# An attention and gating kernel on one core: a rewritten order table, work moved from GpSimd to VectorE, and the inverse transform's third products split off

## The chip, the cores and the metric

The kernel runs on one core of one Trainium2 chip. The metric is the device time of one execution in microseconds (us), the median of a few runs. Lower is better. The engines are called as the profile calls them: PE (TensorE, matrix products; PEld is its weight load), DVE (VectorE), ACT (ScalarE), POOL (GpSimd) and SP (the engine that issues most DMA transfers; its queue is SPq).

## What is computed

Two layers, one behind the other. The first is a linear attention with a learned feature map; the second projects the attention's output three ways, convolves one of the projections with a filter along the sequence by way of a Fourier transform, multiplies the three, and projects once more.

```python
# q, k, v: (8, 8, 576, 64); w_phi: (64, 128)
def phi(x):
    proj = einsum('bhsd,df->bhsf', x, w_phi)
    proj = proj - max(abs(proj), axis=-1)
    return concatenate([exp(proj), exp(-proj)], axis=-1)
q_p, k_p = phi(q), phi(k)
kv = einsum('bhsf,bhsd->bhfd', k_p, v)
num = einsum('bhsf,bhfd->bhsd', q_p, kv)
den = einsum('bhsf,bhf->bhs', q_p, sum(k_p, axis=2)) + 1e-06
x = (num / den) -> (8, 576, 512)          # heads side by side
x1, x2, x3 = split(x @ w_proj, 3)         # w_proj: (512, 1536)
conv = irfft(rfft(x2, axis=1) * rfft(filter, axis=0), axis=1)
out = (x1 * conv * x3) @ w_out            # (8, 576, 512), float32
```

## The kernel before

**An order written out by hand.** The program has no loops over batches that set its order. A long table of words, `PLAN`, is walked once, and each word calls one method with its arguments: `Pk,2,0@0` calls `Pk(2, 0)` with PSUM bank 0. A word issues between one and 72 instructions of one engine. So `PLAN` fixes, for each engine, the order of its instructions; each engine then runs its own list in that order and waits on semaphores where an input or a buffer is not ready. Nothing is moved at run time: an instruction that waits holds back all that stands behind it on its engine. The order of the words that belong to different engines against each other matters only where it decides which of two uses of a buffer comes first.

**One batch.** The 8 batches run through the same stages, overlapped by hand; a batch's words carry its number `b` first.

- Loads: `load,q,b`, `load,k,b`, `load,v,b` (line 596) are issued by POOL, with a cast from float32 to bf16 on the way. Batch 0 is loaded in four halves for q and k instead (`loadh`, line 602). The three column blocks of `w_proj` are loaded by POOL as `w_load,proj,0` to `2` (line 586); block 0 feeds the words `X1`, block 1 `X2`, block 2 `X3`.
- `trh,k,b,X` and `trh,q,b,X` (line 608) transpose one half of k or q by DMA, issued by SP. Batch 0's are transposed on PE (`pt`, line 618) and copied out of PSUM by `pte` on ACT or DVE.
- `Pk` and `Qn` (lines 636, 643) multiply by `w_phi`; `maxk` and `maxq` (DVE, line 716) take the largest magnitudes; `ex` (ACT, line 698) takes the exponentials, 128x1024 at a time. `mhi`, `mlo`, `trm`, `trme` turn the maxima of q so that `Pq` (lines 670, 676) can subtract them in PSUM.
- `em` (ACT) writes the factors of v, and `vs` (line 758) scales v by them: four words per batch, `p` and `m`, two halves X. `KV` (line 773) sums k against scaled v, `KVe` copies it out, `NE` and `NEt` (lines 787, 796) multiply by q, `rc` and `xn` (DVE) divide.
- `trx` (SP, line 825) transposes the attention's output for the projections `X1` and `X3` (line 917). `f1` and `f2` (lines 854, 860) are the two stages of folds, sums and differences of bf16 blocks of 128x512, ahead of the forward Fourier products `Ft` and `Fs` (lines 869, 876). `Fe` and `Xl` copy the spectrum out, `X2` (line 895) projects it, `Y1` (DVE) multiplies by the filter's spectrum into four tiles `T0` to `T3` and a leftover tile `T4`; `m3` (line 909) adds them in pairs.
- `I` (line 970) is the inverse transform of one block of 128 features: six matmuls of 288 columns, three for the even and three for the odd half. `Ie`, `Ip`, `Im` bring it out, `ym` (line 1005) multiplies by the other two projections, `O` (line 1016) is the last projection, `Oe` copies it out, `st` stores it.

**Two shapes of product on PE.** Some words work on 64 rows of the array and pair two halves of a tile (`Pk`, `Qn`, `Pkt`, `Qnt`, `Pq`, `Pqt`, `KV`, `Ft`); the profile writes `64*128` for them. The rest use all 128 rows (`128*128`).

**The third pair of `I`.** `T4` holds the leftover frequencies, 64 rows of the even and 64 of the odd half; the tile `inv` holds zeros in the rows of the other half. So `I` multiplies all 128 rows of `T4` once for each half.

**Set-up.** Before the first batch POOL writes index tables (`gi_nr`, `gi_fr` and others, lines 322 to 342), DVE and ACT turn them into angles (`ang`, `frac`) and sines (`sin`), which are the transform's matrices. The filter is loaded by SP (`fl_load`), folded by POOL (`fa`, line 495) into `fs`, and transformed once (`Ff`, `Ffe`, `H`, `He`). `fs` lies in the memory of `turn`, the tile that the sines are computed from. `wz` are products of zeros that fill PE early on. After the set-up, `late` gives its memory to the tiles of the second layer.

Of the kernel before, what the change touches and what calls it, by code (L numbers as in the profile page):

```python
# [36 lines left out]
fl_load,1,1 pt,k,0,1,1@7 exz ex,k,m,0,1@2 maxk,0,0@4 maxq,0,1@0 fl_load,3,1 fl_load,2,0 ex,k,p,0,0@4
pt,k,0,1,0@0 load,v,0 ex,k,m,0,0@4 pt,q,0,1,1@1 load,k,1 fl_load,3,0 maxk,0,1@2 pte,ACT,k,0,1,1@7
fl_load,1,0 pte,DVE,q,0,1,0@6 pte,ACT,k,0,1,0@0 Qn,0,0@4 pte,ACT,q,0,1,1@1 load,q,1 fa,POOL,0
maxq,0,0@4 Pkt,0@6 Qn,0,3@0 trh,k,1,0 maxkt,0@6 ex,k,p,0,1@2 wz,24@4 wz,17@2 trh,q,1,0 Qnt,0@4  # L40
maxq,0,3@0 fa,POOL,1 em,p,0,0 exkt,p,0@6 Pk,0,2@0 exkt,m,0@6 Qn,0,2@2 ex,k,p,0,2@0 maxqt,0@4
Pk,0,3@6 maxq,0,2@2 em,m,0,0 ex,k,m,0,3@6 w_load,proj,2 mhi,0 ex,k,p,0,3@6 rev@4 maxk,0,2@0
vs,POOL,p,0,0 mlo,POOL,0 vs,POOL,m,0,0 ex,k,m,0,2@0 trm,0@2 trme,DVE,0@2 Pq,0,0@2 ex,q,p,0,0@2
Pq,0,1@0 maxk,0,3@6 fb,0@4 em,m,0,1 em,p,0,1 vs,POOL,p,0,1 fb,1@4 wz,11@6 wz,9@7 KV,0,0@6
ex,q,p,0,1@0 ex,q,m,0,1@0 ex,q,m,0,0@2 Pq,0,3@4 Pq,0,2@0 ex,q,m,0,3@4 KVe,DVE,0,0@6 vs,POOL,m,0,1
NE,0,0@6 rc,0,0@6 NE,0,1@2 xn,0,0@6 trh,q,1,1 ex,q,p,0,3@4 Ff,2@6 Pk,1,1@4 rc,0,1@2 xn,0,1@2
f1,POOL,0,0,0 maxk,1,1@4 ex,q,p,0,2@0 Ffe,ACT,2@6 KV,0,1@2 Qn,1,0@6 ex,q,m,0,2@0 wz,5@0
KVe,ACT,0,1@2 ex,k,m,1,1@4 Pk,1,0@2 maxq,1,0@6 ex,k,p,1,1@4 maxk,1,0@2 NE,0,3@0 rc,0,3@0 Ff,3@6
Ffe,ACT,3@6 NE,0,2@4 xn,0,3@0 trh,k,1,1 w_load,proj,0 ex,k,m,1,0@2 Ff,1@6 rc,0,2@4 ptx,0,3@0
xn,0,2@4 ex,k,p,1,0@2 ptx,0,0@1 ptxe,DVE,0,0@1 ptx,0,2@4 f1,POOL,0,0,1 ptxe,DVE,0,3@0 Qnt,1@2  # L50
ptxe,ACT,0,2@4 Ffe,ACT,1@6 maxqt,1@2 Pqt,0@0 exqt,p,0@0 exqt,m,0@0 Qn,1,3@4 Ff,0@6 Ffe,ACT,0@6
Qn,1,2@2 maxq,1,3@4 Pk,1,2@0 Qn,1,1@4 load,v,1 maxq,1,2@2 ex,k,m,1,2@0 maxq,1,1@4 trx,0,1 X1,0,3@6
load,k,2 Pkt,1@2 ex,k,p,1,2@0 w_load,proj,1 maxk,1,2@0 exkt,m,1@2 X1,0,2@7 maxkt,1@2 X1,0,1@4
X1e,ACT,0,2@7 X1e,ACT,0,3@6 mhi,1 NEt,0@0 H,0@5 rct,0@0 xnt,0,1@0 X3,0,1@6 H,3@7 X1e,ACT,0,1@4
f1,POOL,0,1,1 f1,POOL,0,1,0 em,p,1,0 xnt,0,0@0 f2,POOL,0,1,0 tm,0,1@6 load,q,2 f2,POOL,0,1,1
exkt,p,1@2 Ft,0,1,0@2 He,DVE,3,0@7 Fs,0,2@2 Hl,ACT He,DVE,3,1@7 Fs,0,3@0 X1,0,0@4 Fe,ACT,0,2@2
Fe,ACT,0,3@0 Ft,0,0,6@2 He,DVE,0,0@5 X1e,ACT,0,0@4 He,DVE,0,1@5 Pk,1,3@0 f2,POOL,0,0,0 f2,POOL,0,0,1
Fs,0,1@6 Fe,DVE,0,1@6 Fs,0,0@2 H,1@4 ex,k,m,1,3@0 Fe,ACT,0,0@2 He,ACT,1,1@4 X3,0,2@5 He,ACT,1,0@4
mlo,POOL,1 trm,1@6 maxk,1,3@0 em,m,1,0 Xl,DVE,0 trme,DVE,1@6 em,p,1,1 X3,0,0@7 H,2@2 X2,0,2@3
em,m,1,1 ex,k,p,1,3@0 tm,0,0@7 H,4@4 trh,k,2,0 He,DVE,4,0@4 tm,0,2@5 vs,POOL,p,1,0 Pq,1,0@6  # L60
He,ACT,2,0@2 X3,0,3@0 tm,0,3@0 ex,q,m,1,0@6 vs,POOL,m,1,0 KV,1,0@4 vs,POOL,p,1,1 trxt,0
vs,POOL,m,1,1 trh,k,2,1 ex,q,p,1,0@6 Pk,2,0@0 KVe,ACT,1,0@4 Pk,2,1@6 ex,k,p,2,1@6 ex,k,m,2,1@6
trh,q,2,0 late X2,0,3@2 Y1,0,2@3 trh,q,2,1 maxk,2,0@0 X1t,0@3 Y1,0,3@2 maxk,2,1@6 load,v,2 Pq,1,2@4
X1te,ACT,0@3 X2,0,0@3 Y1,0,0@3 X3t,0@2 tmt,0@2 X2,0,1@6 load,q,3 X2,0,4@7 Y1,0,1@6 ex,q,p,1,2@4
Pq,1,1@2 ex,k,p,2,0@0 ex,k,m,2,0@0 Y1,0,4@7 w_load,out ex,q,m,1,2@4 Qn,2,1@0 maxq,2,1@0 ex,q,p,1,1@2
ex,q,m,1,1@2 KV,1,1@4 load,k,3 Qnt,2@6 Pkt,2@0 Pqt,1@2 maxqt,2@6 maxkt,2@0 m3,POOL,0,1 KVe,ACT,1,1@4
exqt,p,1@2 Qn,2,0@6 NE,1,1@4 exqt,m,1@2 maxq,2,0@6 m3,POOL,0,0 rc,1,1@4 xn,1,1@4 I,0,2@2 em,p,2,0
NE,1,0@6 Ie,0,2@2 Im,0,2@2 rc,1,0@6 Ip,0,2@2 exkt,m,2@0 exkt,p,2@0 xn,1,0@6 I,0,0@4 Qn,2,2@2
Ie,0,0@4 Ip,0,0@4 I,0,3@0 vs,POOL,p,2,0 Pq,1,3@6 trh,q,3,1 Ie,0,3@0 ex,q,p,1,3@6 Im,0,0@4
ex,q,m,1,3@6 ym,POOL,0,2 Qn,2,3@4 maxq,2,2@2 Im,0,3@0 I,0,1@2 Ip,0,3@0 maxq,2,3@4 ym,POOL,0,0  # L70
f1,POOL,1,0,0 Ie,0,1@2 Im,0,1@2 NE,1,3@0 rc,1,3@0 Pk,2,3@4 Ip,0,1@2 ym,POOL,0,3 xn,1,3@0 NEt,1@6
trx,1,0 mhi,2 mlo,POOL,2 ex,k,m,2,3@4 NE,1,2@2 em,m,2,0 trm,2@0 trx,1,1 trme,ACT,2@0 Pq,2,1@0
rct,1@6 trh,q,3,0 ex,k,p,2,3@4 ym,POOL,0,1 vs,POOL,m,2,0 xnt,1,0@6 rc,1,2@2 xnt,1,1@6 xn,1,2@2
O,0,1@6 O,0,3@7 trx,1,3 maxk,2,3@4 Pk,2,2@4 ex,q,m,2,1@0 ex,q,p,2,1@0 Oe,DVE,0,1@6 ex,k,p,2,2@4
Qn,3,3@2 Pq,2,2@0 ex,k,m,2,2@4 f1,POOL,1,0,1 maxq,3,3@2 O,0,2@6 Oe,ACT,0,2@6 Oe,ACT,0,3@7
f1,POOL,1,1,1 maxk,2,2@4 load,q,4 KV,2,0@2 KVe,DVE,2,0@2 O,0,0@6 Qn,3,2@4 trx,1,2 Oe,DVE,0,0@6
maxq,3,2@4 Pq,2,0@2 f1,POOL,1,1,0 ex,q,p,2,2@0 X1,1,2@7 ex,q,m,2,2@0 ex,q,m,2,0@2 f2,POOL,1,0,1
trh,k,3,1 X1,1,3@6 ex,q,p,2,0@2 X1e,ACT,1,2@7 st,SP,0,2,1 em,m,2,1 Ft,1,0,4@0 f2,DVE,1,0,0
f2,DVE,1,1,1 f2,DVE,1,1,0 em,p,2,1 X1e,DVE,1,3@6 Fs,1,0@0 Fs,1,1@4 Ft,1,1,2@6 Fs,1,2@6 Fe,ACT,1,0@0
vs,POOL,p,2,1 Fs,1,3@2 st,SP,0,0,1 Fe,DVE,1,2@6 trh,k,3,0 Fe,ACT,1,1@4 trxt,1 NE,2,1@0 rc,2,1@0  # L80
xn,2,1@0 Fe,ACT,1,3@2 X2,1,3@4 Y1,1,3@4 X3,1,2@2 X2,1,0@3 load,k,4 tm,1,2@2 Y1,1,0@3 NE,2,0@4
Pq,2,3@0 ex,q,p,2,3@0 rc,2,0@4 xn,2,0@4 vs,POOL,m,2,1 Qn,3,0@6 ex,q,m,2,3@0 X2,1,2@2 f1,POOL,2,0,0
f1,POOL,2,0,1 maxq,3,0@6 Y1,1,2@2 KV,2,1@4 Pk,3,1@6 X1,1,0@0 KVe,ACT,2,1@4 maxk,3,1@6 NE,2,2@2
st,SP,0,3,0 rc,2,2@2 X2,1,1@1 NE,2,3@4 xn,2,2@2 Xl,ACT,1 X1e,ACT,1,0@0 X1,1,1@0 trx,2,0 Y1,1,1@1
st,SP,0,3,1 ex,k,p,3,1@6 X2,1,4@2 rc,2,3@4 load,k,5 st,SP,0,1,1 ex,k,m,3,1@6 trx,2,2 m3,POOL,1,1
st,SP,0,2,0 Pqt,2@6 st,SP,0,1,0 X1e,ACT,1,1@0 exqt,m,2@6 Pk,3,0@0 m3,POOL,1,0 trx,2,1 xn,2,3@4
trx,2,3 Pkt,3@4 Y1,1,4@2 maxkt,3@4 f2,POOL,2,0,1 X3,1,3@3 maxk,3,0@0 exqt,p,2@6 exkt,p,3@4
exkt,m,3@4 X1t,1@2 X1te,ACT,1@2 f1,POOL,2,1,0 I,1,3@6 tm,1,3@3 X3t,1@4 I,1,1@2 Ie,1,3@6 em,p,3,0
ex,k,m,3,0@0 X3,1,0@5 Ie,1,1@2 load,v,3 Im,1,3@6 Ip,1,3@6 I,1,0@6 tmt,1@4 Im,1,1@2 Ip,1,1@2 Ie,1,0@6
ym,POOL,1,3 trh,q,4,1 st,SP,0,0,0 tm,1,0@5 Im,1,0@6 trh,q,4,0 ex,k,p,3,0@0 Ip,1,0@6 X3,1,1@3 NEt,2@4  # L90
tm,1,1@3 rct,2@4 xnt,2,1@4 I,1,2@0 Qnt,3@2 xnt,2,0@4 Pk,3,2@6 ym,POOL,1,1 maxqt,3@2 Ie,1,2@0
Im,1,2@0 Ip,1,2@0 ym,POOL,1,0 X1,2,0@0 ym,POOL,1,2 Pk,3,3@2 Qn,3,1@4 ex,k,m,3,2@6 X1e,ACT,2,0@0
ex,k,p,3,2@6 X1,2,2@1 maxq,3,1@4 X1,2,1@0 mhi,3 f1,POOL,2,1,1 load,v,4 O,1,2@4 maxk,3,3@2
X1e,ACT,2,1@0 Oe,ACT,1,2@4 em,m,3,0 X1e,DVE,2,2@1 trh,k,4,0 maxk,3,2@6 f2,POOL,2,0,0 ex,k,p,3,3@2
O,1,3@0 O,1,0@1 mlo,POOL,3 f2,POOL,2,1,1 f2,POOL,2,1,0 Ft,2,0,6@4 Fs,2,1@6 Oe,ACT,1,0@1 Oe,DVE,1,3@0
Fe,DVE,2,1@6 ex,k,m,3,3@2 X3,2,0@0 tm,2,0@0 trm,3@1 Fs,2,0@4 O,1,1@2 Oe,DVE,1,1@2 vs,POOL,p,3,0
st,SP,1,2,1 vs,POOL,m,3,0 Fe,ACT,2,0@4 trme,ACT,3@1 Qnt,4@4 trh,k,4,1 Ft,2,1,0@6 Fs,2,3@0
Fe,ACT,2,3@0 Fs,2,2@6 em,m,3,1 Pq,3,1@2 vs,POOL,m,3,1 ex,q,m,3,1@2 maxqt,4@4 load,q,5 Qn,4,0@4
Fe,DVE,2,2@6 Pq,3,0@0 ex,q,p,3,0@0 X2,2,3@6 em,p,3,1 ex,q,p,3,1@2 trxt,2 ex,q,m,3,0@0 maxq,4,0@4
Y1,2,3@6 X3,2,1@7 tm,2,1@7 X2,2,2@4 Y1,2,2@4 Xl,ACT,2 trh,k,5,1 KV,3,0@2 Qn,4,2@0 KVe,ACT,3,0@2  # L100
maxq,4,2@0 Pq,3,2@4 Pk,4,1@6 ex,q,m,3,2@4 maxk,4,1@6 X2,2,0@2 ex,q,p,3,2@4 NE,3,1@0 rc,3,1@0
X2,2,1@3 ex,k,p,4,1@6 vs,POOL,p,3,1 xn,3,1@0 ex,k,m,4,1@6 KV,3,1@4 KVe,ACT,3,1@4 Pq,3,3@0 Y1,2,1@3
# [994 lines left out]
```

## Time and profile before

| | |
|---|---|
| median of 3 runs | 293.58 us (292.82 to 296.74) |
| span of the profiled execution | 291.2 us |
| the runs' median less that span | 2.4 us |
| PE busy | 274.0 us, 94%, 4336 matmuls |
| DVE busy | 252.3 us, 87% |
| POOL busy | 228.5 us, 78% |
| ACT busy | 221.9 us, 76% |
| PE's granted clock | 0.996 |

The time of the profiled execution is its span, from the first to the last instruction, and what lies around it; the runs that were timed are other executions. In the profile's rows a group is written `line engine operation out<-in shapes xcount`. A row of the timeline begins with the start and the duration in us, and names in brackets how long the engine was idle before and who released it. A row of the table of windows gives a stretch, then the busy time and the number of instructions of PE, PEld, DVE, ACT and POOL in it, the granted clock, the mean busy share of the DMA engines, and GB/s.

### The profile page before, as it was taken

To read this page: it belongs to the slowest core of one execution; us is meant where nothing else is said; L and a number is where in the kernel's file an instruction comes from. 1 tells how busy PE (TensorE), PEld (TensorE's weight loads), DVE (VectorE), ACT (ScalarE), POOL (GpSimd) and SP (SyncE) were. 2 spreads that over 40 slices of the span, in tenths; PEclk is the share of its full clock that TensorE was granted. 3 is DMA by queue.
4 is the path that set the end of the run, shared out by engine and by line. 5 is a ranking of instruction groups with operands and counts; after the bars stand their busy time and mean duration, and the time that the engine had idled before them with its cause. 6 is when DMAs were issued, how large, how long until landed. Compare 5 with 4: busy or idle time off the path is not lost.

```text
span 291.2 us, 10275 instructions
## 1 busy us (share of the span) xinstructions
PE 274.0 (94%) x4336; PEld 194.8 (67%) x4336; DVE 252.3 (87%) x438; ACT 221.9 (76%) x367; POOL 228.5 (78%) x187
## 2 busy tenths in 40 slices
...
GB/s 140 230 207 175 144 204 165 139 175 181 143 192 177 163 204 159 153 119 165 122 111 156 197 169 114 163 135 191 99 14 93 84 36 2 34 108 54 69 130 184
DMA packets 72319, 40.07 MB, mean 138 GB/s; under 512 B 52496, under 2 KB 67216, under 8 KB 72272
## 3 DMA queue, kind: packets, MB, share of 16 engines
...
q10 hardware_dynamic: 320, 0.52, 0.7%
...
HBM read 33.75 MB, written 9.44 MB: 148 GB/s over the span
## 4 chain that ended last, share of the span: by engine, by line
PE 71%; DVE 3%; ACT 2%; issue 1%; DVEq 0%; ACTq 0%
PE ps L917 17%; PE ps L895 11%; PE ps L1016 10%; PE ps L970 8%; PE ps L773 5%; PE ps L787 4%; PE ps L876 3%; PE ps L926 2%; PE ps L670 2%; PE ps L636 2%; PE ps L643 2%; PE ps L676 2%; PE ps L869 2%; DVE mq L716 1%; PE ps L796 1%
## 5 line engine op out<-in xcount | busy, mean ns | idle before, releaser
L917 PE MATMUL ps<-xT,wproj 128*128 128x256 bf16 x512 | 64.0, 273 | 0.2 <-DMA wproj<-in_moe_w_proj_dram 0.2
L917 PEld LDWEIGHTS <-wproj 128*128 128x128 bf16 x512 | 48.1, 98 | 9.0 <-DMA wproj<-in_moe_w_proj_dram 0.4
L1005 POOL TENSOR_TENSOR yT<-cv,x1s 128x576 bf16<-128x576 f32 x31 | 39.4, 1279 | 15.6 <-ACT es L988 7.7
L716 DVE TENSOR_REDUCE mq<-ps 128x8 f32<-128x1024 f32 (+1 forms) x40 | 43.7, 1112 | 3.5 <-PE ps L643 1.5
L716 DVE TENSOR_REDUCE mk<-ps 128x8 f32<-128x1024 f32 (+1 forms) x40 | 44.1, 1112 | 2.9 <-PE ps L636 1.6
L758 POOL TENSOR_TENSOR vm<-vn,vm 128x1152 bf16<-128x1152 bf16 x16 | 34.3, 2152 | 7.4 <-ACT vm L752 7.4
L758 POOL TENSOR_TENSOR vp<-vn,vp 128x1152 bf16<-128x1152 bf16 x16 | 34.4, 2155 | 4.6 <-ACT vp L752 4.5
L698 ACT ACTIVATE Eqp<-ps 128x1024 bf16<-128x1024 f32 x32 | 32.9, 1038 | 6.1 <-PE ps L676 6.0
L854 POOL TENSOR_TENSOR SD<-xn 128x512 bf16<-128x512 bf16 x28 | 31.9, 1153 | 6.2 <-DVE xn L806 4.7
L1016 PE MATMUL ps<-wout,yT 128*128 128x512 bf16 x140 | 34.8, 379 | 0.1
L860 POOL TENSOR_TENSOR xf<-SD 128x512 bf16<-128x512 bf16 x26 | 29.7, 1155 | 6.4 <-DVE SD L854 5.9
L698 ACT ACTIVATE Ekp<-ps 128x1024 bf16<-128x1024 f32 x32 | 33.2, 1036 | 1.1 <-PE ps L636 0.7
L698 ACT ACTIVATE Eqm<-ps 128x1024 bf16<-128x1024 f32 x32 | 32.6, 1037 | 1.6 <-PE ps L676 0.8
L698 ACT ACTIVATE Ekm<-ps 128x1024 bf16<-128x1024 f32 x32 | 33.1, 1033 | 0.8 <-PE ps L636 0.7
L895 PE MATMUL ps<-wproj,XF 128*128 128x512 bf16 x128 | 31.6, 379 | 0.3 <-ACT x1s L298 0.3
L991 DVE TENSOR_TENSOR cv<-es,ps 128x288 f32<-128x288 f32 x64 | 26.3, 445 | 5.7 <-ACT es L988 4.4
L909 POOL TENSOR_TENSOR T<-T,T 128x1024 bf16<-128x1024 bf16 x14 | 29.6, 2127 | 1.7 <-DVE r L801 0.8
L970 PE MATMUL ps<-inv,T 128*128 128x288 bf16 x192 | 28.1, 286 | 0.7 <-DVE mq L716 0.4
L958 DVE TENSOR_TENSOR x1s<-ps,x1s 128x512 bf16<-128x512 f32 x32 | 21.8, 685 | 2.5 <-PE ps L917 1.1
L298 ACT COPY o<-ps 128x512 f32<-128x512 f32 x20 | 11.8, 600 | 14.4 <-PE ps L1016 12.0
L806 DVE TENSOR_TENSOR xn<-ps,r 128x512 bf16<-128x512 f32 x32 | 21.9, 689 | 0.9
L298 ACT CAST x1s<-ps 128x512 bf16<-128x512 f32 (+1 forms) x33 | 17.4, 540 | 6.7 <-PE ps L917 3.2
...
## 6 DMA issues: line engine op xcount, KB each, us to landing
...
vn<-in_v_dram POOLq DMA_DIRECT2D x8, 576.0 KB, 7.8
kn<-in_k_dram POOLq DMA_DIRECT2D x7, 576.0 KB, 7.8
qn<-in_q_dram POOLq DMA_DIRECT2D x7, 576.0 KB, 7.2
wproj<-in_moe_w_proj_dram POOLq DMA_DIRECT2D x3, 512.0 KB, 8.7
...
```

The source lines that it names most:

```text
L298: self.nc.scalar.copy(dst, src)
L698: self.nc.scalar.activation(e, p, AF.Exp, bias=0.0, scale=1.0 if g == "p" else -1.0)
L716: self.nc.vector.tensor_reduce(out=out, in_=src, axis=AX.X, op=ALU.max, apply_absolute_value=True)
L758: self.eng(eng).tensor_tensor(out=t[:, :, :, 0:64], in0=self.at("vn", b)[:, 2 * X:2 * X + 2], in1=t[:, :, :, 64:65].to_broadcast([128, 2, ...
L854: self.eng(eng).tensor_tensor(out=o[:, :, 2 * i:2 * i + 2, :], in0=x[:, :, 0:2, :], in1=x[:, :, 2:4, :], op=ALU.subtract if i else ALU.add)
L860: self.eng(eng).tensor_tensor(out=o[:, :, 2 * i:2 * i + 2, :], in0=x[:, :, 0:4:2, :], in1=x[:, :, 1:4:2, :], op=ALU.subtract if i else ALU ...
L895: self.mm(self.pb(0), l, w[:, kt, 512:1024], start=(kt == 0), stop=(kt == 3))
L909: self.eng(eng).tensor_tensor(out=Y, in0=Y, in1=self.at(f"T{2 * e + 1}", b), op=ALU.add)
L917: self.mm(o[:, d], w[:, kt, f0 + 128 * m:f0 + 128 * m + 128], y[:, 1, ::-1, ::-1] if d else y[:, 0], start=(kt == 0), stop=(kt == 3))
L970: self.mm(self.pb(e, 0, 288), l, inv[:, 2 * e + i if i < 2 else 4 + e, :], start=(i == 0), stop=(i == 2))
L1005: self.eng(eng).tensor_tensor(out=self.at("yT", b)[:, m, 0:SEQ], in0=self.turn_of("cv", (b, m)).rearrange("p x h t -> p (x h t)"), in1=sel ...
L1016: self.mm(self.pb(0), y[:, kt, 128 * c:128 * c + 128], w[:, kt, :], start=(kt == 0), stop=(kt == 3))
```

## The change

**The table.** `PLAN` is replaced as a whole. Most words stay, in nearly the same order; nearly all lines of the table differ. Of such lines:

```diff
-loadh,k,0,0 gi_fr ang,DVE,2 wz,23@0 wz,30@1 wz,31@0 wz,32@1 wz,33@0 ang,ACT,3 fl_loadt ident frac,3
+wz,18@5 ident fl_load,0,1 gi_nr cols_a gi_fr wz,34@7 wz,32@5 cz,DVE,0 loadh,q,0,0 fl_load,2,0 wz,9@1
```

Words that change their engine, counted over the table: `vs` 2 from POOL to DVE (`vs,DVE,p,7,0` and `p,7,1`); `ym` 4 and `m3` 3 from POOL to DVE; `f1` one fewer on DVE, `f2` as many on DVE as before, in other places; `Fe` 3, `Xl` 3, `KVe` 2, `Ffe`, `ptxe`, `X1te`, `trme` and `yt` one each from ACT to DVE; `pte` 2 from ACT to DVE; `Oe` 4, `He` 3 and `X1e` 2 from DVE to ACT.

**The inverse transform.** `I` becomes `Is` (the four matmuls of `T0` to `T3`) and, apart from it, either `Iz` (the third pair as before) or `It` (64 rows of `T4` for each half). Of 32 blocks 23 use `Iz` and 9 `It`. Whichever stands first in the table opens the sum. `Fs` and `Ft` may likewise now come in either order.

```diff
+    def opens(self, *key):
+        new = key not in self.opened
+        self.opened.add(key)
+        return new
...
-    def I(self, b, m):
-        c, inv = slice(128 * m, 128 * m + 128), self.at("inv")
-        for e in range(2):
-            Y = self.at(f"T{2 * e}", b)
-            for i in range(3):
-                l = Y[:, i, c] if i < 2 else self.at("T4", b)[:, c]
-                self.mm(self.pb(e, 0, 288), l, inv[:, 2 * e + i if i < 2 else 4 + e, :],
-                        start=(i == 0), stop=(i == 2))
...
     def It(self, b, m):
+        c, inv, new = slice(128 * m, 128 * m + 128), self.at("inv"), self.opens("I", b, m)
         for e in range(2):
             r = slice(64 * e, 64 * e + 64)
+            self.mm(self.pb(e, 0, 288), self.at("T4", b)[r, c], inv[r, 4 + e, :], start=new,
+                    stop=not new)
+
+    def Iz(self, b, m):
+        c, inv, new = slice(128 * m, 128 * m + 128), self.at("inv"), self.opens("I", b, m)
+        for e in range(2):
+            self.mm(self.pb(e, 0, 288), self.at("T4", b)[:, c], inv[:, 4 + e, :], start=new,
+                    stop=not new)
 
     def Is(self, b, m):
+        c, inv, new = slice(128 * m, 128 * m + 128), self.at("inv"), self.opens("I", b, m)
         for e in range(2):
             for i in range(2):
                 self.mm(self.pb(e, 0, 288), self.at(f"T{2 * e}", b)[:, i, c],
+                        inv[:, 2 * e + i, :], start=new and i == 0, stop=not new and i == 1)
```

**The filter sums.** `fs` no longer lies in `turn` but in a tile of its own, `fsx`, whose first part holds the index tables `fr` and `nr` until the angles are computed:

```diff
-        self.fs = self.turn.rearrange("p a x -> p (a x)")[:, 0:2048].rearrange(
-            "p (a x) -> p a x", a=4)
+        self.fsx = s.tile([128, 2048], FP32, name="fsx")
+        self.fs = self.fsx.rearrange("p (a x) -> p a x", a=4)
...
-        self.fr = s.tile([128, 2, 2, 144], FP32, name="fr")
+        self.fr = self.fsx[:, 0:576].rearrange("p (a b x) -> p a b x", a=2, b=2)
...
-        self.nr = s.tile([128, 288], FP32, name="nr")
+        self.nr = self.fsx[:, 576:864]
```

On ACT the first words are now `ang,ACT,3`, `sin,9`, `sin,2`, `sin,3`, `sin,0`, where `sin,9` stood first, and the program holds three loads of ACT's function table in place of two: one each ahead of `ang`, of `sin` and of the first `ex`.

**What moves, at three places.** In the rows below a name ends in the number of its buffer. POOL's list, from its first load; `raw`, `part`, `idx`, `nr` and `fr` are index tables, `qn_76` and `kn_78` batch 0's q and k. Before:

```order
L602 DMA qn_76<-in_q_dram 128x2x576
L342 ISA
L342 IOTA nr 128x256
L344 IOTA nr 128x32
...
L390 MEMSET raw 1x1
L602 DMA kn_78<-in_k_dram 128x2x576
L332 IOTA fr 128x288
...
L327 IOTA idx_277 128x128
L602 DMA qn_76<-in_q_dram 128x2x576
L602 DMA kn_78<-in_k_dram 128x2x576
```

The same stretch of POOL's list in the changed program, where `nr` and `fr` are parts of `fsx`:

```order
L383 IOTA raw 128x4
...
L337 IOTA fsx 128x256
L339 IOTA fsx 128x32
L327 IOTA fsx 128x288
...
L332 MEMSET fsx 128x1
L597 DMA qn_76<-in_q_dram 128x2x576
L322 IOTA idx_248 128x128
L597 DMA kn_78<-in_k_dram 128x2x576 x2
L597 DMA qn_76<-in_q_dram 128x2x576
```

The first load of q now stands behind the index tables, and the second half of k ahead of the second half of q.

POOL's list a little later: the first `vs`, the blocks of `w_proj` (`wproj_65`), and batch 1's v (`vn_81`) and batch 2's k (`kn_78`). Before:

```order
L495 TENSOR_TENSOR turn<-fl 128x1024 x2
L586 DMA wproj_65<-in_moe_w_proj_dram 128x4x512
L758 TENSOR_TENSOR vp_105<-vn_80,vp_105 128x18x64
...
L758 TENSOR_TENSOR vm_120<-vn_80,vm_120 128x18x64
L854 TENSOR_TENSOR SD_137<-xn_130 128x2x256
L586 DMA wproj_65<-in_moe_w_proj_dram 128x4x512
L854 TENSOR_TENSOR SD_137<-xn_130 128x2x256
L596 DMA vn_81<-in_v_dram 128x4x576
L596 DMA kn_78<-in_k_dram 128x4x576
```

In the changed program:

```order
L490 TENSOR_TENSOR fsx<-fl 128x1024 x2
L591 DMA qn_77<-in_q_dram 128x4x576
L753 TENSOR_TENSOR vp_105<-vn_80,vp_105 128x18x64
...
L753 TENSOR_TENSOR vp_106<-vn_80,vp_106 128x18x64
L581 DMA wproj_65<-in_moe_w_proj_dram 128x4x512 x2
L591 DMA vn_81<-in_v_dram 128x4x576
L591 DMA kn_78<-in_k_dram 128x4x576
L849 TENSOR_TENSOR SD_137<-xn_130 128x2x256
L581 DMA wproj_65<-in_moe_w_proj_dram 128x4x512
```

Block 2 of `w_proj` was loaded ahead of the `vs`; now it stands behind them and behind block 0, in front of batch 1's v and batch 2's k. The first fold (`SD_137`) stands behind these loads.

PE's list where batch 4's inverse transform begins its block 2 (`T_1163`, `T_1165`, `T_1167` are the sums and the leftover tile). Before, behind the last product of `Fs`:

```order
L876 MATMUL ps<-D_67,xf_138 128x144
L970 LDWEIGHTS T_1163
L970 MATMUL ps<-inv_69,T_1163 128x288
L970 LDWEIGHTS T_1163
L970 MATMUL ps<-inv_69,T_1163 128x288
L970 LDWEIGHTS T_1167
L970 MATMUL ps<-inv_69,T_1167 128x288
L970 LDWEIGHTS T_1165
```

In the changed program (`T_1140` is the leftover tile, line 970 is `It`, line 983 `Is`), behind a product of k:

```order
L631 MATMUL ps<-wphi_62,kT_84 128x128
L970 LDWEIGHTS T_1140
L970 MATMUL ps<-inv_69,T_1140 128x288
L970 LDWEIGHTS T_1140
L970 MATMUL ps<-inv_69,T_1140 128x288
L983 LDWEIGHTS T_1136
L983 MATMUL ps<-inv_69,T_1136 128x288
```

The leftover products stand first and are of 64 rows, next to other products of 64 rows. Over the whole list the changes between words of 64 and of 128 rows number 146 before and 164 now; up to the third `O` of batch 0 there are 42 and 56, behind it 104 and 108.

346 lines of the change are left out of this document (169 added, 177 removed).

## Prediction

> **What bounds the kernel now.** I read the page first, then the table of windows, then the timelines of PE and POOL where the windows show a hole.
>
> The table of windows gives the program, whose span ends at 291.20, by stages.
>
> ```profile
> 0.00:40.00 40.00, 31.60 (x508) 19.36 (x509) 34.54 (x94) 35.42 (x54) 31.02 (x41) 1.00 1.14 181
> 40.00:80.00 40.00, 37.71 (x688) 27.77 (x687) 37.77 (x59) 36.50 (x64) 35.33 (x28) 1.00 1.16 165
> 80.00:220.00 140.00, 139.98 (x2228) 101.58 (x2226) 125.59 (x192) 110.67 (x186) 120.83 (x89) 1.00 0.95 148
> 220.00:240.00 20.00, 19.07 (x338) 13.91 (x336) 18.40 (x33) 17.51 (x28) 15.21 (x14) 1.00 0.35 61
> 240.00:280.00 40.00, 40.00 (x560) 29.68 (x555) 32.06 (x57) 20.16 (x36) 26.08 (x18) 1.00 0.28 59
> 280.00:291.20 11.20, 5.66 (x30) 2.54 (x27) 3.91 (x8) 1.66 (x3) 0.00 (x0) 0.90 0.66 167
> 53.00:64.00 11.00, 9.95 (x243) 7.08 (x236) 11.00 (x13) 10.57 (x15) 10.88 (x9) 1.00 1.15 163
> ```
>
> From 80 to 280 us PE is idle for 0.95 us in 200, all but 0.02 of it between 220 and 240. There no other order of the same products can win more than that; only fewer or cheaper products help, and any new wait costs its full length. PE's real holes are in the first 40 us (8.4 us), in the next 40 (2.3) and behind 280, where the last results are copied out and stored (5.5). In the first 80 us other engines lead: the last row shows DVE busy for all of 53 to 64 us.
>
> Inside the full stretch PE's time depends on which shapes stand side by side.
>
> ```profile
> 99.79 0.90 PE L970 MATMUL ps<-inv,T 128*128 128x288 bf16 x6
> 100.53 1.04 PE L917 MATMUL ps<-xT,wproj 128*128 128x256 bf16 x8
> 101.40 0.22 PE L796 MATMUL ps<-KVs,Fqp 128*128 128x130 bf16 x1
> ...
> 103.14 1.05 PE L917 MATMUL ps<-xT,wproj 128*128 128x256 bf16 x8
> 104.11 0.40 PE L636 MATMUL ps<-wphi,kT 64*128 64x128 bf16 x8
> ...
> 109.14 0.42 PE L869 MATMUL ps<-Dt,xnt 64*128 64x288 bf16 x4
> 109.48 0.42 PE L876 MATMUL ps<-D,xf 128*128 128x144 bf16 x4
> ```
>
> From start to next start the same eight matmuls of line 917 take 0.87 us ahead of 128-row products (100.53 to 101.40) and 0.97 ahead of 64-row ones (103.14 to 104.11): a change of shape costs 0.10 us.
>
> **The split inverse.** The six matmuls of `I` take 0.74 us (99.79 to 100.53), 0.123 each, 0.245 for the third pair. Four 64-row matmuls of the same 288 columns (line 869) take 0.34 us with one change of shape in it, so 0.24 for four: two halves run side by side, a pair costs 0.12. Each `It` saves 0.12 us, nine of them 1.1. `Is` and `Iz` cost what `I` cost. Against it stand 18 more changes of shape in PE's list. Four lie behind the third `O` of batch 0 (at about 76 us), where PE is full: 0.4 us. Fourteen lie before it, where PE has holes that hide them; if that cover is gone they cost 1.4. Bounds: a gain of 1.1, a loss of 1.8 less 0 to 1.1. I take -0.7, since the late places are those without holes.
>
> **The start.** POOL's first load moves behind the index tables.
>
> ```profile
> 1.25 0.89 POOL L602 DMA_DIRECT2D qn<-in_q_dram  x1 [0.80 <-POOLq L1081]
> 2.23 0.40 POOL L342 IOTA nr<- 128x256 f32 x1
> ...
> 3.22 0.76 POOL L602 DMA_DIRECT2D kn<-in_k_dram  x1
> 3.99 0.41 POOL L332 IOTA fr<- 128x288 f32 x1
> ...
> 4.92 0.24 POOL L327 IOTA idx<- 128x128 f32 x1
> ```
>
> ```profile
> 12.74 1.01 ACT L698 ACTIVATE Ekm<-ps 128x1024 bf16<-128x1024 f32 x1
> ```
>
> The tables take 2.23 to 3.22 and 3.99 to 4.92, 1.92 us; q's first half is issued 1.9 us later. The first half of k is issued at 1.25 + 1.92 + 0.98 + 0.19 = 4.3 instead of 3.22: 1.1 us later, and with it the first exponential (12.74). The true delay lies between 0 (the filter's loads, now ahead, leave the DMA engines free sooner) and 1.9. I take 1.1. The third table load adds little:
>
> ```profile
> 0.74 1.28 ACT L460 ACT_TABLE_LOAD   x1 [0.74 <-PEq L1081]
> 2.03 0.21 ACT L460 ACTIVATE sz<-zz 128x1 bf16<-128x1 bf16 x1
> ```
>
> 1.28 us, with the next instruction 0.01 behind. It now falls between the angles and the sines, in front of the last sine and the load for the exponentials; alone it would put the first exponential at 12.74 + 1.28 = 14.0, against 13.8 by k's delay, and the two don't add up. The Trainium skill (ScalarE: Activation LUTs, section What ACT_TABLE_LOAD costs) gives about 2.66 us for every switch, a drain of 1.38 included. The trace of this kernel shows 1.28 and no drain behind it. By the page's figure the start would be some 1.4 us later still, an estimate.
>
> ACT then runs almost without a gap, and the change takes work from it: `pte` two fewer (0.6 each), one `ptxe` and one `Ffe` (0.6 and 0.7). That repays 2.5 us by 40 us, less what DVE, which gets them at 0.4 to 0.75 each, holds back through its reductions. At the first projection I expect +0.7 or less. That term is swallowed by the next one.
>
> **The loads behind the first scalings.** This is the term that I take to decide.
>
> ```profile
> 27.06 2.15 POOL L758 TENSOR_TENSOR vm<-vn,vm 128x1152 bf16<-128x1152 bf16 x1
> 30.15 1.16 POOL L854 TENSOR_TENSOR SD<-xn 128x512 bf16<-128x512 bf16 x1 [0.93 <-DVE xn L806]
> 31.25 0.81 POOL L586 DMA_DIRECT2D wproj<-in_moe_w_proj_dram  x1
> ...
> 33.95 0.75 POOL L596 DMA_DIRECT2D kn<-in_k_dram  x1
> ```
>
> The tables of DMA issues in narrow windows give the time to landing of `w_proj` block 0 and of batch 2's k; batch 1's v goes between them.
>
> ```profile
> wproj<-in_moe_w_proj_dram POOLq DMA_DIRECT2D x1, 512.0 KB, 8.2
> kn<-in_k_dram POOLq DMA_DIRECT2D x1, 576.0 KB, 11.2
> ```
>
> ```profile
> 45.28 2.28 SPq L608 DMA_TRANSPOSE kT<-kn  x1
> DMA to landing us min/median/max: 5.9/7.0/8.1
> 53.42 0.62 PE L636 MATMUL ps<-wphi,kT 64*128 64x128 bf16 x16
> ```
>
> Block 0 lands at 39.45 and k at 45.15, with v between them: two slots of 2.85 us, for loads that were issued 2.70 apart (31.25 and 33.95). So the queue is at its throughput. In the change block 2 of `w_proj` joins it in second place, so batch 2's k lands one slot, 2.8 us, later. Against that POOL reaches block 0 sooner: behind the last `vs` (29.21) and not behind a wait of 0.93 and a fold of 1.16, up to 2.05 us sooner, less the delay of `vs` itself, whose factors hang on the late start (1.1 to 2). So k lands 0.75 to 2.8 us later. SP starts its transposition the moment k is there (45.28), it lands at most 8.1 us later, at 53.38, and PE uses it at 53.42. There is no slack. PE, then `maxk` on DVE, then all behind it wait; with DVE busy for 11.00 of 11 us there, nothing takes the delay up. If the transposition took the other row's 5.9 us, none of it would be left. I take +2.0, from 0 to 2.8.
>
> **What is hidden.** The prices on the two engines:
>
> ```profile
> L909 POOL TENSOR_TENSOR T<-T,T 128x1024 bf16<-128x1024 bf16 x14 | 29.6, 2127 | 1.7 <-DVE r L801 0.8 <-DVE T L905 0.8
> L909 DVE TENSOR_TENSOR T<-T,T 128x1024 bf16<-128x1024 bf16 x2 | 1.3, 683 | 0.0
> L1005 POOL TENSOR_TENSOR yT<-cv,x1s 128x576 bf16<-128x576 f32 x31 | 39.4, 1279 | 15.6 <-ACT es L988 7.7 <-DVE cv L991 5.4 <-DVE x1s L958 1.7
> L1005 DVE TENSOR_TENSOR yT<-cv,x1s 128x576 bf16<-128x576 f32 x1 | 0.8, 759 | 0.0
> ```
>
> `m3` costs 0.68 us on DVE and 2.13 on POOL, `ym` 0.76 and 1.28. No row has `vs` on DVE: between 0.77 (`m3` scaled from 1024 to 1152 elements) and POOL's 2.15; I take 0.9. With three `m3`, four `ym`, two `vs` and the copies, less `Oe`, `He` and `X1e`, DVE gets some 8 us more. From 80 to 220 us it is free for 14 of 140, from 240 to 280 for 8 of 40, so PE, which leads there, covers it: cost 0, and up to 8 if it all fell where DVE is full. The two `vs` of batch 7 finish sooner, but PE has no hole from 240 to 280 for that to fill. The filter sums of their own start before the sines are done; POOL's two sums end ahead of the product that needs them either way. The end keeps its form, the last projection, six copies, ten stores: 0, within 0.4.
>
> **The sum.** 291.2 + 2.0 - 0.7 = 292.5 us of span; with the 2.4 us by which the runs' median stands above the profiled span, **294.9**.
>
> **The rivals.** *Nothing is late (0.30).* POOL reaches the loads two microseconds sooner and the queue, then less crowded by transpositions, makes up the slot; ACT's relief shows. Then 291.2 - 0.7 and half a microsecond of the hole at 220, and 2.4: 292.4. For it: 0.75 is the lower end of k's delay and the two transposition rows differ by 2.2. Against: no slack at 53.4.
>
> *Slower (0.13): DVE becomes the bound.* Place: the folds, `m3`, spectrum copies and `KVe` of batches 3 to 5, 120 to 215 us, where a late DVE holds `NE`, `X2` and `Is` on PE. It decides from the point where PE shows more than 4 us of idle time between 80 and 220. Price: 8 us of DVE work less nothing hidden, with the late k: 291.2 + 2.0 - 0.7 + 6 + 2.4 = 300.9. Against it: 14 us free there.
>
> *The 64-row products don't overlap, and each change of shape counts (0.07):* 0 instead of -1.1, +1.8 instead of 0.4: 294.9 + 2.5 = 297.4. Against: line 869.
>
> *Clearly faster (0.05):* the holes at 40 to 80 (2.3) and 220 to 240 (0.9) close, the head gains ACT's 2.5, the split 0.7: 291.2 - 6.4 + 2.4 = 287.2.
>
> **How the numbers follow.** The forecast has 0.45. About 2% (5.9 us) is what a measurement of this kernel can tell from no change. Faster takes the last rival and a little of the first: 0.06. Slower takes the DVE rival, and the forecast's upper tail: 0.13. The rest, 0.81, is within 2%. The range goes from the first rival with all the bounds in its favour (290.3) to the forecast with the largest delay and the loss of the split (299.0); the DVE rival's half above that, and half of the clear gain, are left out.
>
> **What would show it.** Right: PE idle some 2 us more between 40 and 60, at the first product of batch 2's k (line 631 there), ended by the DMA into `kT`; the load of k landing near 47.5; `It` pairs of 0.12 us; PE's 80 to 220 still at 140 of 140. Wrong: that product on time, or new idle time of PE behind DVE after 80 us, or a PE total for the same stretch that moves by more than 1 us.

## The result and the profile after

The changed kernel takes 301.96 us (median of 5 runs, 301.62 to 304.75) against 293.58: slower by 2.8% (ratio 1.0283, 95% interval 1.0223 to 1.0343), 8.4 us. The forecast was 294.9, the range 290.3 to 299.0.

The profiled execution is the slowest of the five, 304.75 us with a span of 302.9; the run with the median has 300.2. The rows of the table of windows from 80 us on, of the changed kernel:

```profile
80.00:220.00 140.00, 134.11 (x2172) 97.81 (x2193) 128.99 (x195) 106.82 (x173) 112.41 (x85) 1.00 0.92 146
220.00:240.00 20.00, 18.46 (x377) 14.51 (x372) 18.78 (x32) 16.10 (x24) 13.60 (x11) 1.00 0.29 60
240.00:280.00 40.00, 38.32 (x548) 26.49 (x553) 36.31 (x54) 25.84 (x44) 23.74 (x18) 1.00 0.31 57
```

The stretch from 80 to 220 us, in which PE had no hole, now has 5.9 us of them (134.11 of 140), and from 240 to 280 there are 1.7. (21 matmuls have no record there, 2172 against 2193 weight loads. They leave 20 holes of 0.05 to 0.16 us; without these 4.7 us of the 5.9 stay.) The view of PE's waits, in us in total, times and the longest, names the releasers; of its rows these are the longest behind 80 us:

```profile
PE ps L768 <- issue: 1.6, 1, 1.6
PE ps L897 <- DVE T L907: 1.3, 2, 1.0
...
PE ps L919 <- DVE o L295: 0.8, 1, 0.8
...
PE ps L976 <- DVE cv L990: 0.7, 1, 0.7
...
PE ps L1015 <- DVE xnt L813: 0.6, 1, 0.6
PE ps L878 <- DVE xf L855: 0.5, 1, 0.5
```

Apart from the first row it is DVE each time. The groups of DVE's instructions show why. Of before:

```profile
L860 DVE TENSOR_TENSOR xf<-SD 128x512 bf16<-128x512 bf16 x6 | 2.3, 416 | 0.0
...
L300 DVE COPY yT<-yT 128x256 bf16<-128x256 bf16 x1 | 0.2, 216 | 0.0
```

The same operations in the changed kernel:

```profile
L1004 DVE TENSOR_TENSOR yT<-cv,x1s 128x576 bf16<-128x576 f32 x5 | 5.2, 1032 | 0.1
L855 DVE TENSOR_TENSOR xf<-SD 128x512 bf16<-128x512 bf16 x6 | 4.7, 783 | 0.0
...
L753 DVE TENSOR_TENSOR vp<-vn,vp 128x1152 bf16<-128x1152 bf16 x2 | 4.0, 2012 | 0.0
L849 DVE TENSOR_TENSOR SD<-xn 128x512 bf16<-128x512 bf16 x3 | 2.7, 891 | 0.1
L295 DVE COPY yT<-yT 128x256 bf16<-128x256 bf16 x2 | 2.4, 1192 | 0.0
```

A fold of the same shape takes 0.78 and 0.89 us in the mean where it took 0.42, the small copy `yt` 1.19 where it took 0.22. One place at a time, the timelines of POOL, DVE and PE of the changed kernel around 141 us:

```profile
140.86 1.29 POOL L1004 TENSOR_TENSOR yT<-cv,x1s 128x576 bf16<-128x576 f32 x1
```

```profile
140.82 0.44 DVE L990 TENSOR_TENSOR cv<-es,ps 128x288 f32<-128x288 f32 x1
141.19 1.26 DVE L855 TENSOR_TENSOR xf<-SD 128x512 bf16<-128x512 bf16 x1
142.36 0.44 DVE L990 TENSOR_TENSOR cv<-es,ps 128x288 f32<-128x288 f32 x1
```

```profile
141.90 0.29 PE L976 MATMUL ps<-inv,T 128*128 128x288 bf16 x1
142.86 0.28 PE L976 MATMUL ps<-inv,T 128*128 128x288 bf16 x1 [0.67 <-DVE cv L990]
```

POOL's product runs to 142.15. The fold that DVE starts at 141.19 ends at 142.45, 0.30 us behind it: it waits for POOL, and then does its work. The `cv` behind it comes late, the PSUM bank that it frees comes late, and PE stands for 0.67 us. The `cv` ahead of it, with one operand in SBUF and one in PSUM, ran beside POOL's product in its usual 0.44.

The same around 250 us, with one of the scalings that the change gave to DVE:

```profile
248.92 2.15 POOL L753 TENSOR_TENSOR vm<-vn,vm 128x1152 bf16<-128x1152 bf16 x1 [0.62 <-ACT vm L747]
```

```profile
249.62 2.67 DVE L753 TENSOR_TENSOR vp<-vn,vp 128x1152 bf16<-128x1152 bf16 x1
252.21 0.28 DVE L295 COPY XL<-XF 128x512 bf16<-128x512 bf16 x1
252.41 1.35 DVE L753 TENSOR_TENSOR vp<-vn,vp 128x1152 bf16<-128x1152 bf16 x1
253.68 2.34 DVE L907 TENSOR_TENSOR T<-ps,HTo 128x1024 bf16<-128x1024 f32 x2
```

The first ends at 252.29, 1.22 us behind POOL's `vm` (251.07); the second meets nobody and takes 1.35. `Y1` behind them starts at 253.68, and PE waits 1.05 us for it (254.94). Going through the folds, `m3`, `ym`, `yt` and `vs` on DVE, which read SBUF alone: in the kernel before there are 14, and none met a sum or product of POOL. In the changed kernel there are 23, with 22.4 us; unheld (0.42 for a fold, 0.68 `m3`, 0.76 `ym`, 0.22 `yt`, 1.35 `vs`) they would take 14.1. So DVE stands for **8.3 us** in such holds, and the five waits of PE above, from 0.5 to 1.0 (3.6 us together), each stand right behind one. `Xl`, a copy within SBUF that the change puts on DVE four times in place of once, adds 0.6 us: one of the four met a product of POOL and took 0.86, the others 0.28. The Trainium skill (SBUF — State Buffer, section SBUF: two separate sides) has the rule: VectorE and GpSimd share a pair of ports, whichever starts first holds it for its whole instruction, and a VectorE instruction with two inputs in SBUF is one that needs it. This trace agrees, but for one start:

```profile
113.14 2.59 POOL L753 TENSOR_TENSOR vp<-vn,vp 128x1152 bf16<-128x1152 bf16 x1
```

```profile
113.31 0.40 DVE L855 TENSOR_TENSOR xf<-SD 128x512 bf16<-128x512 bf16 x1
```

The fold that began 0.17 us behind POOL's scaling was not held, and the scaling took 2.59 us where the one above took 2.15. The run `part_back` below shows how little decides this.

### The profile page after: what moved, and what is told of

Its sections match the earlier page's. It is cut to its first block, busy times and chain, and to the rows that moved or that the text cites. A ratio compares the mean times of both kernels' runs of the same rounds, so it can differ in the third digit from the quotient of the medians.

```text
span 302.9 us, 10242 instructions
## 1 busy us (share of the span) xinstructions
PE 275.9 (91%) x4303; PEld 195.5 (65%) x4336; DVE 267.6 (88%) x452; ACT 223.6 (74%) x362; POOL 217.2 (72%) x179
## 4 chain that ended last, share of the span: by engine, by line
PE 58%; DVE 22%; ACT 7%; DMA 5%; issue 4%; POOL 2%; DVEq 0%; ACTq 0%; POOLq 0%
PE ps L919 13%; PE ps L897 9%; PE ps L1015 8%; PE ps L768 5%; DVE mq L711 4%; PE ps L782 4%; DVE mk L711 4%; PE ps L983 3%; DMA kT<-kn 3%; DMA kn<-in_k_dram 3%; DVE cv L990 2%; PE ps L878 2%; DVE xn L801 2%; PE ps L638 2%; PE ps L631 2%
## 5 line engine op out<-in xcount | busy, mean ns | idle before, releaser
L1004 POOL TENSOR_TENSOR yT<-cv,x1s 128x576 bf16<-128x576 f32 x27 | 34.8, 1299 | 16.1 <-DVE cv L990 13.6
L849 POOL TENSOR_TENSOR SD<-xn 128x512 bf16<-128x512 bf16 x29 | 33.3, 1164 | 14.6 <-DVE xn L801 14.1
L753 POOL TENSOR_TENSOR vp<-vn,vp 128x1152 bf16<-128x1152 bf16 x14 | 30.6, 2186 | 8.5 <-ACT vp L747 6.1
L911 POOL TENSOR_TENSOR T<-T,T 128x1024 bf16<-128x1024 bf16 x11 | 23.3, 2127 | 17.5 <-DVE T L907 17.5
L1015 PE MATMUL ps<-wout,yT 128*128 128x512 bf16 x126 | 33.5, 379 | 1.5 <-DVE xnt L813 0.6
L897 PE MATMUL ps<-wproj,XF 128*128 128x512 bf16 x115 | 30.6, 379 | 1.2 <-issue 0.3
L855 POOL TENSOR_TENSOR xf<-SD 128x512 bf16<-128x512 bf16 x26 | 30.4, 1190 | 0.6
L987 ACT COPY es<-ps 128x288 f32<-128x288 f32 x32 | 12.8, 405 | 19.0 <-PE ps L983 6.8
L293 ACT CAST x1s<-ps 128x512 bf16<-128x512 f32 (+1 forms) x34 | 18.4, 547 | 11.0 <-PE ps L919 7.9
L1015 PEld LDWEIGHTS <-yT 128*128 128x128 bf16 x140 | 12.8, 97 | 14.0 <-issue 1.1
```

Of the source, the lines that this page charges most:

```text
L753: self.eng(eng).tensor_tensor(out=t[:, :, :, 0:64], in0=self.at("vn", b)[:, 2 * X:2 * X + 2], in1=t[:, :, :, 64:65].to_broadcast([128, 2, ...
L849: self.eng(eng).tensor_tensor(out=o[:, :, 2 * i:2 * i + 2, :], in0=x[:, :, 0:2, :], in1=x[:, :, 2:4, :], op=ALU.subtract if i else ALU.add)
L855: self.eng(eng).tensor_tensor(out=o[:, :, 2 * i:2 * i + 2, :], in0=x[:, :, 0:4:2, :], in1=x[:, :, 1:4:2, :], op=ALU.subtract if i else ALU ...
L897: self.mm(self.pb(0), l, w[:, kt, 512:1024], start=(kt == 0), stop=(kt == 3))
L911: self.eng(eng).tensor_tensor(out=Y, in0=Y, in1=self.at(f"T{2 * e + 1}", b), op=ALU.add)
L1004: self.eng(eng).tensor_tensor(out=self.at("yT", b)[:, m, 0:SEQ], in0=self.turn_of("cv", (b, m)).rearrange("p x h t -> p (x h t)"), in1=sel ...
```

## The experiments

The changes to the table are shown by a word or two of each kind.

**Order and engines apart.** `order_only` undoes the engines, `engines_only` does them alone, `sbuf_back` undoes them for the words that read SBUF alone.

```diff
-f1,DVE,1,1,1  vs,DVE,p,7,0  Fe,DVE,1,1@4  Oe,ACT,0,0@7
+f1,POOL,1,1,1 vs,POOL,p,7,0 Fe,ACT,1,1@4  Oe,DVE,0,0@7
```

> The changed kernel with its order of words, its split inverse and its filter tile, but each of the 82 words whose engine the change moved is put back on its old engine. Theory E (the changed engines cost the time: VectorE has 15 us more to do, half of it because its folds, its sums of two SBUF tensors, now run while GpSimd runs its own): 294 to 296 us, that is the late start of 2 us and little else. Theory O (the new order costs it, whichever engine does the work): 300 to 303 us. Theory S (the split inverse and its changes of shape cost it): also 300 to 303, and the run with the split alone slower by 4 or more.

> The kernel before with its own order, and the 82 words put on the engines of the changed kernel. Theory E: 298 to 302 us, the folds and scalings on VectorE taking 0.8 us and more wherever GpSimd works at the same time. Theory O: 293 to 295.

> The changed kernel with only the words of two SBUF operands (scalings of v, folds, m3, ym, yt) on their old engines; the copies out of PSUM stay where the change put them. Theory E in its form 'VectorE and GpSimd hold each other up': most of what the whole set of engines is worth comes back, 296 to 298 us. Theory E in its form 'VectorE simply has more work': about half of it, 298 to 300. Theory O: 300 to 303.

Measured 315.06 (ratio 1.0686, 1.0599 to 1.0772), 323.75 (1.0988, 1.0903 to 1.1074) and 305.63 (1.0396, 1.0317 to 1.0476). All three missed. The new order with the old engines is slower than either kernel, and the old order with the new engines slower still: the two parts of the change were fitted to each other, and undoing one says nothing on what the other costs. In `sbuf_back` the holds of these words are nearly gone (0.8 us left by the same sum). But POOL, which needs 1.16 us for a fold that costs DVE 0.42, is late in their place: PE waits 3.0 us for its folds and its `ym`. `Xl`, which stays on DVE there, is held for 3.3 us, and two stalls marked "issue" (told of below) take 3.3. So the question had to be asked without moving work.

**The holds alone.** `no_hold` leaves order and engines as changed, and lets 18 words on DVE (`vs`, folds, `ym`, `yt`) read one operand. Each becomes a reduction over one element, so their sums and products are left out, and with them the wait of `vs` for its factors; `yt`, a copy, becomes one too. The five `m3` stay as they are.

```diff
+    def single(self, o, x):
+        self.nc.vector.tensor_reduce(out=o, in_=x.unsqueeze(len(x.shape)), axis=AX.X, op=ALU.max)
...
     def f1(self, eng, b, h, i):
+        if eng == "DVE":
+            return self.single(o[:, :, 2 * i:2 * i + 2, :], x[:, :, 0:2, :])
```

> The changed kernel, in which VectorE's share of the scalings of v, of the folds, of ym and of yt reads only one of its operands in SBUF (a reduction over a single element in place of the sum or product, so the arithmetic of these 18 words is left out); same order, same engines, same sizes, and each still waits for the same inputs save the factors of v. Theory H (these words wait in VectorE until GpSimd's running instruction has ended, 8.3 us in all, and five of PE's stalls behind 80 us, 3.6 us together, stand right behind such a wait): their durations become independent of GpSimd, 0.3 to 1.3 us each by size, and the time falls by 3 to 5 us to 297 to 299. Theory L (VectorE just has more to do, held or not): the durations unheld are as before, so 301 to 302. Theory D (the order alone costs): 301 to 302.

298.02 us, ratio 1.0124 (1.0082 to 1.0166), which does not reach the changed kernel's interval: 1.6% or 4.7 us of the 8.4 are gone (2.5 to 6.8 by the two intervals). The two profiled executions bear out the lower end. Their spans differ by 5.6 us (302.9 and 297.3), of which 3.0 lie ahead of the first fold on DVE (it starts at 81.86 and 78.87), where none of the 18 words has run yet; 2.6 us are gone behind it. POOL is freed with DVE: its scaling that took 2.59 takes 2.15. DVE's groups in this kernel:

```profile
L752 DVE TENSOR_REDUCE xf<-SD 128x512 bf16<-128x512 bf16 x6 | 4.0, 675 | 0.0
...
L752 DVE TENSOR_REDUCE yT<-yT 128x256 bf16<-128x256 bf16 x2 | 0.8, 382 | 0.0
```

A fold's stand-in costs 0.68, more than an unheld fold, and the kernel is faster all the same. Around the same fold as above DVE and PE read

```profile
138.23 0.68 DVE L752 TENSOR_REDUCE xf<-SD 128x512 bf16<-128x512 bf16 x1
138.82 0.44 DVE L999 TENSOR_TENSOR cv<-es,ps 128x288 f32<-128x288 f32 x1
```

```profile
138.94 0.66 PE L985 MATMUL ps<-inv,T 128*128 128x288 bf16 x2
139.44 0.65 PE L992 MATMUL ps<-inv,T 128*128 128x288 bf16 x4
```

with POOL's product running beside it from 137.88 for 1.29 us as before. The fold no longer waits, and PE no longer stands.

**DVE's own work.** `to_act` has ScalarE do the 18 words as copies (`self.nc.scalar.copy(o, x)` in `single`); `before_vs` puts the two scalings alone on DVE in the kernel before; `part_back` takes them, and `yt`, off DVE in the changed one.

> The changed kernel with VectorE's 18 words of scalings, folds, ym and yt done by ScalarE as copies of one operand (their arithmetic is left out), at the same places of the order. Theory L (VectorE's own extra work, without any hold, costs part of what is left): 294.5 to 296.5. If only the holds cost: 297 to 299, as in the run without holds. If ScalarE becomes late with 8 us more: over 299.

> The kernel before with only the two scalings of batch 7 put on VectorE. Theory H: each takes 1.35 us plus the rest of GpSimd's scaling that is then running, up to 2.15, where VectorE is in front of Y1, which PE waits for: 295 to 298. By the prediction's reading (VectorE is free there, cost 0): 293 to 294.5.

> The changed kernel with the two yt on VectorE back on ScalarE and the two scalings of batch 7 back on GpSimd, nothing else. Theory H: PE's stalls at 239 (0.76 us) and 253 us (1.45) stand behind these words and go, 299.5 to 300.5; if GpSimd, which then has 4.3 us more to do at 245 to 255, becomes late with them, the second stall stays in another form and the time is 301 to 303.

`to_act`: 299.46 (1.0189, 1.0152 to 1.0226), no faster than without holds. Up to 240 us its PE is 1.1 us ahead of `no_hold`'s, and then it waits for ScalarE (`PE ps L665 <- ACT Fqm L705`, 1.3 us). So DVE's unheld work shows as about 1 us there. That is no bound: ScalarE does the words in its place, and `Xl` is still held for 1.9 us in this trace. `before_vs`: 297.73 (1.0112, 1.0075 to 1.0149), 3.3 us slower. The two scalings meet no work of POOL there, and still:

```profile
244.68 1.35 DVE L750 TENSOR_TENSOR vp<-vn,vp 128x1152 bf16<-128x1152 bf16 x1
245.94 0.68 DVE L950 TENSOR_TENSOR x1s<-ps,x1s 128x512 bf16<-128x512 f32 x1
246.54 1.35 DVE L750 TENSOR_TENSOR vp<-vn,vp 128x1152 bf16<-128x1152 bf16 x1
247.81 2.35 DVE L897 TENSOR_TENSOR T<-ps,HTe 128x1024 bf16<-128x1024 f32 x2
```

```profile
246.68 1.02 PE L887 MATMUL ps<-wproj,XF 128*128 128x512 bf16 x4 [0.32 <-DVE x1s L950]
...
250.21 0.43 PE L765 MATMUL ps<-vp,Ekp 64*128 64x65 bf16 x16 [1.52 <-DVE T L897]
```

2.7 us of work stand in front of `Y1`, and PE waits 1.8 of it. That DVE has 8 us free in 40 is no cover for a word that stands in front of one PE waits for. `part_back`: 301.71 (1.0257, 1.0216 to 1.0298), not told apart from the changed kernel by time. The two waits that it aimed at (line 1015 for `xnt`, line 897 for `T`) are gone from its trace, but one of 1.3 us for `xf` at 111 us has come:

```profile
110.33 2.14 POOL L753 TENSOR_TENSOR vp<-vn,vp 128x1152 bf16<-128x1152 bf16 x1
```

```profile
110.55 2.19 DVE L855 TENSOR_TENSOR xf<-SD 128x512 bf16<-128x512 bf16 x1
```

```profile
112.80 0.36 PE L878 MATMUL ps<-D,xf 128*128 128x144 bf16 x3 [1.30 <-DVE xf L855]
```

It is a hold too. This is the fold that escaped in the changed kernel's trace, where it started 0.17 us behind POOL's scaling and took 0.40; here it started 0.22 behind and took 2.19. In four more traces with the same words there (`all_iz`, `head_back`, `loads_late`, `stores_moved`) it started 0.15 to 0.17 behind and took 0.40 or 0.41. Up to there the two programs are the same, so one program can pay a hold in one execution and not in another, and `part_back` does not say what the two words that it moves cost.

**The start, the split and the tile.** `head_back` puts the three loads back:

```diff
-gi_col  ... cz,DVE,0 loadh,q,0,0 ... loadh,k,0,0 ... load,q,1 ... w_load,proj,0 w_load,proj,2
+loadh,q,0,0 gi_col ... gi_nr loadh,k,0,0 ... load,q,1 w_load,proj,2 ... w_load,proj,0
```

`all_iz` writes `Iz` for each `It` of the changed table; `split_only` and `tile_only` are the kernel before with the new tile and `Is` followed by `It` (nine times) or `Iz` where `I` stood.

> The changed kernel with three loads back at their old places: the first half of q ahead of the index tables, the first half of k among them, block 2 of w_proj ahead of the first scalings of v. Theory of the prediction (the late start and the late k of batch 2 cost 2 us): 299.5 to 300.5. If the start is not what costs: 301.5 to 302.5.

> The changed kernel with each of its nine 64-row leftover products of the inverse put back to all 128 rows with zeros, at the same places. By the rows of the kernel before: nine pairs at 0.12 us more, less the changes of shape that go away, so within 1 us of the changed kernel either way. If the 64-row products are what costs (theory S): 298 to 300.

> The kernel before with its own order and engines; the filter sums have their own tile, and the inverse is split, nine blocks with 64-row leftovers at the place where they stood, so that each of them brings two more changes of shape. By the prediction's rows nine times 0.12 us won and 18 changes at 0.10 lost: 293.5 to 295. Theory S: 297 or more.

> The kernel before with its own order and engines, the filter sums and index tables in the new tile, and the leftover products of the inverse called apart but with all 128 rows: the same products on PE as before. If the split with 64 rows is what made the split alone 2 us slower: 293 to 294. If the tile did it: 295 to 296.5.

`head_back`: ratio 1.0279 (1.0221 to 1.0337), as the changed kernel: the start is not what costs. `all_iz`: 302.44 (1.0314, 1.0256 to 1.0372): 0.9 us above the changed kernel, which the intervals don't tell from nothing. `split_only`: 296.47 (1.0078, 1.003 to 1.0127), 1.5 us above what was expected, `tile_only`: 295.86 (1.0059, 1.0018 to 1.0101), as expected if the tile did it: not told apart, so the new tile is enough to explain both, and no cost of the 64-row products shows. Both traces show a hole that the kernel before doesn't have, in the first `X1` of batch 4; of `split_only`:

```profile
168.05 1.69 PE L920 MATMUL ps<-xT,wproj 128*128 128x256 bf16 x14 [1.39 <-DMA xT<-xn]
```

The transposition lands late there. Why the new tile should make it late no run shows. The changed kernel's trace has no such wait, so whether the tile costs anything there stays open.

**A stall that nothing on an engine explains.** The wait of 1.6 us marked "issue" stands inside a `KV` word:

```profile
126.96 0.32 PE L768 MATMUL ps<-vm,Ekm 64*128 64x65 bf16 x10
128.86 0.27 PE L768 MATMUL ps<-vm,Ekm 64*128 64x65 bf16 x6 [1.57 <-issue]
```

Line 768 had its operands: ten such matmuls had just run. Counted through PE's list it is ahead of matmul 1886 (the first is 0), and the queue that the page calls "instruction" moved 34 packets of 16 KB in the whole program, one of them from 126.6 to 127.6. Four runs tried to clear the stretch, by moving two loads or six stores. All four missed what was expected.

```diff
-load,v,4 ... load,k,6 ... m3,POOL,2,0
+m3,POOL,2,0 load,v,4 load,k,6
```

> The changed kernel with two loads, batch 4's v and batch 6's k, moved behind the last m3 of batch 2 in GpSimd's list, out of the stretch from 116 to 126 us in which eight stores and a transposition are under way. Theory F (PE's stall of 1.25 to 1.6 us inside the KV word of batch 3, always ahead of the same matmul, 1886, is a fetch of PE's instructions that comes late behind these transfers): the stall goes to under 0.4 us and the time falls by about 1.3, to 300.3 to 301. If the stall is something in the data or in VectorE's lateness: it stays, 301.5 to 302.5.

> The same move of two loads in the kernel in which VectorE's scalings, folds, ym and yt read one SBUF operand (their arithmetic is left out). Theories H and F together: 298.0 less 1.3, that is 296 to 297. If F is wrong: 298.

> The changed kernel with six of the eight stores that SP issues between 116 and 124 us moved: two of batch 0 ahead to 107, four of batch 1 behind batch 3's transpositions at about 135. Theory F: PE's stall ahead of matmul 1886 falls under 0.5 us and the time by about 1.3, to 300.2 to 301.2, if the stores collide with nothing at their new places; a new stall of batch 3's X1 or batch 5's Qn would show that they do.

> The same move of six stores in the kernel in which VectorE's scalings, folds, ym and yt read one SBUF operand (their arithmetic is left out). Theories H and F together: 296 to 297. If F is wrong: 298.

`loads_late`: the stall ahead of matmul 1886 is gone, the packet begins at 121.6, and the time is 310.44 (1.0577, 1.0533 to 1.062), 8.5 us more. PE's waits say where it went:

```profile
PE ps L919 <- DMA xT<-xn: 3.4, 1, 3.4
PE ps L638 <- DMA qT<-qn: 2.2, 1, 2.2
PE ps L613 <- DMA qn<-in_q_dram: 1.8, 1, 1.8
PE ps L768 <- issue: 1.5, 2, 1.3
```

Two loads, whose data were needed 20 and 30 us later, now ran from 128 to 139 us, beside the transpositions of batch 3's output and of batch 5's q, which landed late; and two more stalls of the "issue" kind came, of 1.3 us at 164 and 1.2 at 171. `no_hold_loads` did the same: 310.13 (1.053, 1.0488 to 1.0572). `stores_moved`: 309.46 (1.0476, 1.0413 to 1.0539), and the stall stays at 1.29; with `no_hold_stores`, 308.67 (1.0399, 1.0334 to 1.0465), it is 0.66, and a wait of 6 us of batch 5's Qn at 145 us, behind the stores, is new. So moving the loads took that stall away and moving the stores did not, and its price could not be won back by either.

## Why the prediction was wrong

- **The step that failed: "What is hidden", cost 0.** Its count of work was near: 8 us estimated for DVE, and 15.3 measured (252.3 to 267.6), 8.9 of them holds with `Xl`, so 6.4 of work. What it lacked is that a price of one engine can hang on what another does at that moment. The rows for the fold, `m3` and `ym` on DVE were all taken while POOL stood still or worked elsewhere, which the view of groups doesn't tell; it would have taken the timelines of both engines side by side. The price of `vs`, which had no row, came out at 1.35 unheld and 2.67 held, not 0.9.
- **The cover.** 14 us free in 140 were taken as cover for 8 us of work. DVE works through a list, and PE waits for single words in it; a late word shows at once, as `before_vs` measured (2.7 us of work put in front of `Y1`, PE waiting 1.8 of it, and 3.3 us more in the time, 2.2 to 4.4 by its interval).
- **The late start and the late k of batch 2, +2.0, taken as deciding: about 0.** In the profiled execution the lag is there. PE's `Pk` of batch 2 starts at 56.48, with 0.94 us of waiting for `kT`, against 53.42 before. But in this execution k's first half landed 1.6 us late (11.8 against 10.2) and the granted clock was 0.74 while PE stood idle. Of the changed kernel:

```profile
10.00:15.00 5.00, 2.85 (x26) 1.37 (x29) 2.27 (x6) 2.43 (x3) 0.80 (x1) 0.74 1.18 228
```

```profile
56.48 0.62 PE L631 MATMUL ps<-wphi,kT 64*128 64x128 bf16 x16 [0.94 <-DMA kT<-kn]
```

And of `all_iz`, which has the same start word for word:

```profile
10.00:15.00 5.00, 4.10 (x50) 2.18 (x49) 4.06 (x9) 4.26 (x6) 1.01 (x1) 1.00 1.18 234
```

```profile
53.23 0.62 PE L631 MATMUL ps<-wphi,kT 64*128 64x128 bf16 x16 [0.32 <-DMA kT<-kn]
```

  Its `Pk` is 0.2 us ahead of the kernel before; its k landed at 44.9 against 45.1. POOL reached block 0 of `w_proj` sooner (29.84 us in `all_iz`, 31.25 before), and from there k took 15.0 us in place of 13.9. So the extra transfer cost 1.1 us and not a slot of 2.8, no more than what POOL had won, which was the first rival's mechanism. `head_back` agrees.
- **The split, -0.7:** neither shown nor refuted; `all_iz` is 0.9 us slower, within noise. Of the 18 changes of shape that the prediction charged to it, `all_iz`, which has none of the 64-row products, still has 16 (162 against 146 in the kernel before), so most came with the new order.
- **The third table load:** of the right size (1.28 us), and hidden as said.
- **The rivals.** "DVE becomes the bound" gave 300.9 and is the one that came nearest, with its sign that PE would show more than 4 us of holes between 80 and 220 (4.7 without the holes of missing records, though 1.6 of these are the stall inside `KV`). That its number lies near is in part luck: it holds the 2.0 of the late k, which did not come, and it names 8 us of DVE work unhidden but adds 6. It was given 0.13, because its mechanism, 8 us of work in places without room, seemed too large for the room that there is. The holds, which double the load, were not in it.
- **The range.** Its upper end is given as the largest delay and the loss of the split, 299.0; these two terms added to the forecast make 298.2. The time lies above either.

**What adds up.** Of 8.4 us 4.7 are the holds by the timed runs of `no_hold`, and 2.6 by its trace; that they cost time is shown, how much only between these. What is left, 3.7 to 5.8, is in part the stall inside `KV` (1.3 in `no_hold`'s trace, and two of 0.4 and 0.5 of its kind) and perhaps 1 us of DVE's own work; the rest, small waits spread over 80 to 280 us, stays open. That the two parts of the change were each worse alone is shown; how far the new order would go with engines fitted to it in another way was not tried.
